# Empty slots of expert 0 written early by plain transfers instead of late by scatters, and the counts read after the last product of the first layer

## The chip, the core and the metric

The kernel runs on one NeuronCore of a Trainium2 chip. The metric is device microseconds of one execution, lower is better; a time is the median of several runs. Engines: PE (TensorE, matmul), DVE (VectorE), ACT (ScalarE), POOL (GpSimd), SP (SyncE, which here only issues transfers). Each engine runs its own instructions strictly in order and waits on semaphores.

## The reference: what is computed

```python
# stage 1, per batch b and head h (8 batches, 8 heads, 576 positions, 64 channels)
scores = q @ k.T / sqrt(64);  ret = scores * gamma_h ** (i - j) for j <= i, else 0
x = (ret @ v), heads side by side           # 4608 tokens x 512
# stage 2, a mixture of 8 experts, one expert a token
logits = x @ w_gate;  e = argmax(logits);  gate_w = softmax(logits)[e]
eom = sigmoid(x @ w_output_gate)
out[token] = gate_w * eom[e] * (relu(x @ w1[e]) @ w2[e])     # w1 512x1024, w2 1024x512
```

The kernel does the two layers of an expert as three products each, of a rounded high half and a low rest of both operands (`w1h`, `w1l`, `xh`, `xl`, `hh`, `hl`).

## The kernel before, in words

**Stage 1, the tile loop.** A loop over 36 tiles g of 128 tokens (two batches are 9 tiles). In tile g PE computes the scores of tile g+1 (`sc`), the part of the output that comes from the running state (`by_state`, `o_ps`), the part from the tile's own scores (`outT`), the state's update (`st_ps`), transposes of k for some tiles (`k_ps`), and, for tile g-1, the transposed result and the gate's logits (`xnat`, `xa` and `xb`). DVE masks the scores (`S_sb`), scales the output (`xT`), adds up logits (`lg`), does the gate, and makes the low half of expert 0's weights (`lo_w`, line 153). POOL scales v (`prep`, tile `vp`, line 364) and issues the scatters. SP loads tile g+4 (`pk`, 768 KB), rows of k (`kn`) and weights (`st`). Order within each of these engines is the order of the code (a manual schedule); a `pk` load waits until its buffer (one of 5) is free.

**The gate and the slots.** Every four tiles form a group n (9 groups). For each token the gate finds its expert and its slot: a running count `cum` per expert (over the groups so far) plus the rank within the group. Expert e owns rows e·4608 and on of a table `xs` in DRAM, 2112 bytes a row: 512 values of x, the token's number and its weight. `gate3a` makes the slots (`sli`), `gate3b` adds four scatters to a list `todo`, each writing 128 token rows to their slots (`scatter_x`); `scatters(n, pause)` takes n of them a tile and issues a small memset (`gap`) ahead of each.

**Slots that stay empty.** The MLP reads 616 slots of every expert, whatever the counts (3 tiles of up to 128, 360 slots in all, then 2 tiles of 128). A slot that got no token must hold zeros and a token number that the output scatter drops. `zx` is 128 such empty rows in SBUF. `fill` computes on DVE the numbers of the slots from the count on (all others are pushed out of range and dropped), and each fill is a scatter of `zx`. Expert 0 starts before the gate is done: its first 360 slots (part 0) hold only tokens of groups 0 to 5 (`SNAP` = 5); if the count after group 5 is below 360, later tokens start at slot 360 (`bump`, `base2`). So part 0 is filled by 3 scatters made in tile 27 (`gate4`, n == SNAP) and issued in tiles 29 and 30, and read in tile 31 (`load_rows`, `load_idx`). Three more scatters, made and issued in tile 35 (n == 7), fill expert 0's part 1, 128 slots each, and the slots of the last group, group 8, wait for them (`gt["after"]`), since its rows go over filled ones. For that count group 7 has five extra small matmuls (`c_ps`, lines 477 and 479).

**Stage 2, the experts.** For each expert the first layer `mm1(e, part, fb)` (8 blocks fb, for part 0 with 360 tokens and part 1 with 256), the second layer `mm2(e, t)` (5 token tiles), then the output scatter (line 299) on POOL. Expert 0's blocks 0 to 4 of part 0 run while the last group's gate is computed. Then come the final counts: a matmul of `cum` (line 738), its copy to `cnt` and the `fill` of all experts on DVE, the fills of experts 1 and 0 on POOL (`fill_slots`), and blocks 5 to 7. (The counts' matmul lies between two hand-ordered sections; on PE it came to stand inside block 5.) The fills of expert e+2 are issued while expert e runs. A read of `xs` waits for every scatter issued in the code ahead of it.

Of the kernel before, what the change touches and what calls it, by code (L numbers as in the profile page):

```python
# [10 lines left out]
F32 = mybir.dt.float32  # L11
# [37 lines left out]
def tile_retention_moe(  # L49
# [80 lines left out]

    wpool.tile([P, 48], F32, name="shift1")
    W1, W2 = {}, {}

    def start_w(which, e, fp):
        src, shape = (w1, [P, KB, 256]) if which == 1 else (w2, [P, 2, DM])
        st = wst.tile(shape, F32, name="st")
        SP.dma_start(out=st, in_=src[e, fp].rearrange("p (a b) -> p a b", a=shape[1]))
        hi = wpool.tile(shape, F32R, name=f"w{which}h{fp}")  # L140
        lo = wpool.tile(shape, F32R, name=f"w{which}l{fp}")
        (W1 if which == 1 else W2)[e, fp] = (hi, lo)
        return st, hi, lo
# [17 lines left out]
    xta.tile([P, 32], F32, name="shift2")  # L161
    XG, XT, HT = {}, {}, {}
    pe = [None]
    scat, todo, fillt = [], [], []
    pools = {"xt0": xta, "ht0": hpa}

    def read(paced=False, first=None, **kw):
# [31 lines left out]
    def scatter_x(x, at, bound=None):  # L199
        i = G.indirect_dma_start(out=xs, out_offset=bass.IndirectOffsetOnAxis(ap=at, axis=0), in_=x, in_offset=None,  # L200
                                 **({} if bound is None else dict(bounds_check=bound, oob_is_err=False)))
        tc.declare_no_dep(i.ins, group="xs", reason="the slots written differ, and those read so far get no more")
        tc.add_to_no_dep_group("xs", i.ins)
        scat.append(i.ins)

    def fill(e0, e1, n, lim, nj, late=False):

# [108 lines left out]
    def load(g):  # L316
        t = ld.tile([P, 3, 512], F32, name="pk")
        SP.dma_start(out=t, in_=pack[g])
        pk[g] = t
# [144 lines left out]
    def gate2(ps):  # L464

        n, oh, ex, zs = gt["pend"]
        r_ps = ps[:, 0:GT * E].rearrange("p (t e) -> p t e", t=GT)
        T.matmul(r_ps, lhsT=cbf_sb[:, 0, :], rhs=oh, start=True, stop=False, skip_group_check=True)
        if n > 0:
            T.matmul(r_ps, lhsT=cbf_sb[:, 1, :], rhs=cum.rearrange("p (a e) -> p a e", a=1).broadcast_to([P, GT, E]),  # L470
                     start=False, stop=False, skip_group_check=True)
        for t in range(GT - 1):
            T.matmul(r_ps[:, t + 1:], lhsT=cbf_sb[:, 1, :], rhs=oh[:, t:t + 1].broadcast_to([P, GT - 1 - t, E]),
                     start=False, stop=t == GT - 2, skip_group_check=True)
        c_ps = ps[:, GT * E:GT * E + E]
        if n in (SNAP, NTILE // GT - 2):
            T.matmul(c_ps, lhsT=cbf_sb[:, 1, :], rhs=cum, start=False, stop=False, skip_group_check=True)
            for t in range(GT):
                T.matmul(c_ps, lhsT=cbf_sb[:, 1, :], rhs=oh[:, t], start=False, stop=t == GT - 1, skip_group_check=True)
        gt["ps"] = (r_ps, c_ps)  # L480

    def gate3a():
        n, oh, ex, zs = gt["pend"]
        r_ps, c_ps = gt.pop("ps")
        bs = base if n <= SNAP else base2
        sl = sm.tile([P, GT, E], F32, name="sl", bufs=1)
        V.tensor_tensor(out=sl, in0=r_ps, in1=bs.broadcast_to([P, GT, E]), op=ALU.add)
        if n in (SNAP, NTILE // GT - 2):
            V.tensor_copy(cnt[:, 0], c_ps[:, 0:1])
        V.tensor_tensor(out=sl, in0=sl, in1=oh, op=ALU.mult)  # L490
        slf = sm.tile([P, GT, 1], F32, name="slf")
        V.tensor_reduce(out=slf, in_=sl, op=ALU.add, axis=AX.X)
        sli = sm.tile([P, GT, 1], I32, name="sli")
        i = V.tensor_copy(sli, slf)
        for j in gt.get("after", ()):
            tc.add_manual_dep(i.ins, j.name, SYNC, reason="the last group's rows go over filled slots")
        gt["sl"] = sli

    def gate3b():
# [16 lines left out]
    def gate3c():  # L516
        n, oh = gt.pop("cum")
        if n == 0:
            V.memset(cum, 0.0)
        ohs = sm.tile([P, E], F32, name="ohs")  # L520
        V.tensor_reduce(out=ohs, in_=oh.rearrange("p t e -> p e t"), op=ALU.add, axis=AX.X)
        V.tensor_tensor(out=cum, in0=cum, in1=ohs, op=ALU.add)
        if n in (SNAP, NTILE // GT - 2):
            gt["fill"] = n

    def gate4():
        n = gt.pop("fill")
        if n == NTILE // GT - 2:

            V.tensor_tensor(out=cnt[:, 0], in0=cnt[:, 0], in1=bump, op=ALU.add)  # L530
            todo.extend(fill(0, 1, cnt[:, 0:1], lim, CT - TA + 1)[0])
        if n == SNAP:

            todo.extend(fill(0, 1, cnt[:, 0:1], float(CA), TA)[0])
            V.tensor_scalar(out=bump, in0=cnt[:, 0], scalar1=-1.0, scalar2=float(CA), op0=ALU.mult, op1=ALU.add)
            V.tensor_scalar(out=bump, in0=bump, scalar1=0.0, scalar2=None, op0=ALU.max)
            V.tensor_copy(base2, base)
            V.tensor_tensor(out=base2[:, 0, 0:1], in0=base2[:, 0, 0:1], in1=bump, op=ALU.add)

    def xnat(g):  # L540
        xa = ps_1.tile([P, 512], F32, name="xa")
# [47 lines left out]
    def scatters(n, pause):  # L589
        for f in todo[0:n]:  # L590

            G.memset(pause, 0.0)
            f()
        del todo[0:n]

    with tc.manual_schedule():
        S_next = scores(0)
        k_rows(0)
        for g in range(NTILE):
            S_sb = S_next  # L600
            prev = stcur[0] if g % CPB != 0 else None
            if g < 4:
                load_rest(g)
            load_k(g + 1)
            if g < NTILE - 4:
                load(g + 4)
            if g == GT * SNAP + 11:
                first = list(scat)
            if g == GT * SNAP + 11:
                for t in range(TA):  # L610
                    load_rows(0, t, first)
                load_idx(0, 0, first)
            if g == 0:
                outT(g, S_sb, prev)
            if g + 1 < NTILE:
                prep(g + 1)
                S_next = scores(g + 1)
            else:
                pools["x_ps"] = k_bank
                transp(0, 2)  # L620
            if g < NTILE - 1:

                scatters(2 if GT * SNAP + 6 < g < GT * SNAP + 11 else 1, gap)
            if prev is not None:
                by_state(g, prev)
            weights(g)
            if g > 0:
                outT(g, S_sb, prev)
            update(g)
            if "pend" in gt and g % GT == 2:  # L630

                gate2(ps_s.tile([P, NP, P], F32, name="k_ps").rearrange("p a i -> p (a i)"))
            if g + 1 < NTILE:
                k_rows(g + 1)

            if "half" in gt:
                gate1b()
            if "fill" in gt:
                gate4()
            if "ps" in gt:  # L640
                gate3a()
            weights_lo(g, (0,))
            weights_lo(g - 1, (1,))
            if g > 0:
                xnat(g - 1)
            if "sl" in gt and g != NTILE - 2:
                gate3b()
            if g % GT == 0 and g > 0:
                gate1a(g // GT - 1)
            if g == NTILE - 1:  # L650
                wide = wk.tile([P, H, D], F32, name="vp")
                gate3c()
                gate4()
                scatters(len(todo), wide)
            if g in (NTILE - 3, NTILE - 2):
                if g == NTILE - 2:
                    pools["x_ps"] = lambda: sc[:, 1].rearrange("p (b k i) -> p b k i", b=2, k=2)
                x = transp_hi(0, g - NTILE + 3)
                if "sl" in gt:
                    gate3b()  # L660
                transp_lo(*x)
    gt["after"] = list(scat)
    psctx.close()
    ps_h = mctx.enter_context(tc.tile_pool(name="ps_h", bufs=4, space=PSUM, side="right", reuse_waits="tile"))
    pools["ps_h"] = ps_h
# [68 lines left out]
    hidden(*block)  # L734
    weights(NTILE)
    weights_lo(NTILE)
    c_ps = ps_t.tile([P, 512], F32, name="t_ps")[:, 0:E]
    T.matmul(c_ps, lhsT=cbf_sb[:, 1, :], rhs=cum, start=True, stop=True)
    V.tensor_copy(cnt[:, :, 0], c_ps)
    V.tensor_tensor(out=cnt[:, 0], in0=cnt[:, 0], in1=bump, op=ALU.add)  # L740
    fills = fill(0, E, cnt, lim, CT)
    fills[0] = fill(0, 1, cnt[:, 0:1], float(CAP), 1, late=True)[0]
    rest.__exit__(None, None, None)

    def fill_slots(e):
# [6 lines left out]
        load_rows(0, t)  # L752
    load_idx(0, 1)
    w = [start_w(1, 1, fp) for fp in range(2)]
    fill_slots(1)
    fill_slots(0)
    for fb in range(5, FB):
        mm1(0, 0, fb)
    load_idx(1, 0)
    load_idx(1, 1)  # L760
    mm2(0, 0)
# [164 lines left out]
```

## Time and profile before

| | |
|---|---|
| median of 3 runs | 603.85 us (603.75 to 605.16) |
| the profiled execution, its own time | 600.12 us |
| its span, first to last instruction | 598.3 us |
| granted PE clock | 0.996 |
| busy: PE, DVE, ACT, POOL | 586.4, 330.8, 227.0, 186.3 us |
| tile loop | up to about 155 us |
| scatters of token rows, of fills | 36, 42 |

In a line of the timeline stand start (us), duration (us), engine, line of the code, operation, tile written <- tiles read, shape, and, in brackets, the idle time of the engine just before and what ended it. Several like instructions in a row are merged (x16), with the duration from the first start to the last end. Ends of matmuls are modelled. In a line of the windows stand the stretch, its length, the busy time of PE, of PE's weight loads, of DVE, ACT and POOL with the number of instructions, the granted clock, the DMA share and GB/s. SPq and POOLq are the issuing sides of these engines.

### The profile page before, as it was taken

The numbers are of one execution on the slowest core, as the hardware profiler recorded it, in microseconds if no ns is written. First come the engines' busy times: TensorE is split into PE (matmuls) and PEld (weight loads), VectorE is DVE, ScalarE is ACT, GpSimd is POOL, SyncE is SP. The second block draws the span as 40 slices with busy tenths as digits, with TensorE's granted clock in tenths as the row PEclk, the third lists the DMA queues.
The fourth block names the chain that finished last, engine by engine and source line by source line (L and its number), as shares of the span: only waits on it lengthen the run. The fifth ranks groups of instructions, "written<-read, shape, count | busy, mean of one in ns | idle before, by whom it ended". The sixth has DMA issues, their size and how long they took to land. (4 is left out here: it accounts for less than half of the span.)

```text
span 598.3 us, 14014 instructions
## 1 busy us (share of the span) xinstructions
PE 586.4 (98%) x5692; PEld 525.7 (88%) x5692; DVE 330.8 (55%) x731; ACT 227.0 (38%) x502; POOL 186.3 (31%) x235
## 2 busy tenths in 40 slices
PE   8999999999999999999999999999999999999995
PEld 6889899889988999889979987997899799889974
DVE  3589899898641864626543472454355435626410
ACT  4534443334322554325333442443344234325210
POOL 3245555575655551125014102501330110110011
PEclk9999999999999999999999999999999999999998
DMA  8889889886235565326424732453273335421011
GB/s 325 293 288 322 323 299 350 328 307 202 92 118 170 173 219 149 141 67 162 172 86 129 183 122 90 125 163 110 89 181 129 121 97 151 131 77 53 1 42 39
DMA packets 54429, 98.97 MB, mean 165 GB/s; under 512 B 14903, under 2 KB 33336, under 8 KB 54364
## 3 DMA queue, kind: packets, MB, share of 16 engines
q1 hardware_dynamic: 44492, 75.42, 39.0%
q0 software_dynamic: 9440, 21.60, 9.9%
q8 instruction: 45, 0.74, 0.5%
q10 hardware_dynamic: 432, 1.05, 0.5%
q14 instruction: 20, 0.16, 0.1%
HBM read 76.45 MB, written 31.18 MB: 180 GB/s over the span
## 5 line engine op out<-in xcount | busy, mean ns | idle before, releaser
L272 PE MATMUL h_ps<-xh,w1h 128*128 128x256 f32 (+1 forms) x512 | 154.7, 302 | 0.0
L272 PE MATMUL h_ps<-xh,w1l 128*128 128x256 f32 (+1 forms) x512 | 154.5, 302 | 0.0
L272 PE MATMUL h_ps<-xl,w1h 128*128 128x256 f32 (+1 forms) x512 | 154.5, 302 | 0.0
L299 POOL DMA_INDIRECT out_dram<-y,idx x40 | 39.8, 995 | 314.3 <-ACT y L298 268.5
L280 DVE SCALAR_TENSOR_TENSOR hl<-h_ps,hh 128x256 fp32r<-128x256 f32 (+1 forms) x128 | 61.1, 477 | 129.1 <-ACT hh L279 125.7
L293 PE MATMUL y_ps<-w2h,hh 128*128 128x512 f32 (+1 forms) x320 | 125.0, 390 | 0.0
L293 PE MATMUL y_ps<-w2l,hh 128*128 128x512 f32 (+1 forms) x320 | 124.9, 390 | 0.0
L293 PE MATMUL y_ps<-w2h,hl 128*128 128x512 f32 (+1 forms) x320 | 124.7, 390 | 0.0
L279 ACT ACTIVATE hh<-h_ps 128x256 fp32r<-128x256 f32 (+1 forms) x128 | 54.8, 428 | 116.9 <-PE h_ps L272 114.8
L272 PEld LDWEIGHTS h_ps<-xh,w1l 128*128 128x128 f32 x512 | 97.1, 190 | 0.0
L272 PEld LDWEIGHTS h_ps<-xh,w1h 128*128 128x128 f32 x512 | 96.1, 188 | 0.3
L272 PEld LDWEIGHTS h_ps<-xl,w1h 128*128 128x128 f32 x512 | 96.1, 188 | 0.3
L298 ACT ACTIVATE y<-y_ps,idx 128x512 f32<-128x512 f32 (+1 forms) x40 | 27.5, 688 | 138.7 <-issue 90.1
L153 DVE TENSOR_TENSOR w1l<-st,w1h 128x512 fp32r<-128x512 f32 x64 | 47.3, 776 | 48.0 <-ACT w1h L148 46.6
L293 PEld LDWEIGHTS y_ps<-w2h,hl 128*128 128x128 f32 (+1 forms) x320 | 58.8, 184 | 14.1
L293 PEld LDWEIGHTS y_ps<-w2h,hh 128*128 128x128 f32 (+1 forms) x320 | 58.8, 184 | 13.7
L293 PEld LDWEIGHTS y_ps<-w2l,hh 128*128 128x128 f32 (+1 forms) x320 | 58.8, 184 | 13.6
L364 POOL TENSOR_TENSOR vp<-pk,con_sb 128x512 f32<-128x512 f32 x36 | 37.5, 1041 | 52.9 <-PE st_ps L404 37.4
L200 POOL DMA_INDIRECT xs<-xgrp,sli x36 | 39.1, 1087 | 29.8 <-issue 12.9
L200 POOL DMA_INDIRECT xs<-zx,fill x42 | 43.3, 1031 | 7.2 <-issue 6.5
L388 DVE TENSOR_TENSOR S_sb<-sc,con_sb 128x512 f32<-128x512 f32 x64 | 41.0, 682 | 7.4 <-PE sc L377 7.0
L153 DVE TENSOR_TENSOR w2l<-st,w2h 128x512 fp32r<-128x512 f32 x64 | 44.7, 736 | 0.0
(130 smaller groups left out, 676.1 us busy)
## 6 DMA issues: line engine op xcount, KB each, us to landing
st<-in_w_dram SPq DMA_DIRECT2D x64, 512.0 KB
pk<-in_pack_dram SPq DMA_DIRECT2D x32, 768.0 KB
x_q<-xs SPq DMA_DIRECT2D x140, 64.0 KB
kn<-in_krow_dram SPq DMA_DIRECT2D x13, 256.0 KB
pk<-in_pack_dram SPq DMA_DIRECT2D x4, 256.0 KB
pk<-in_pack_dram SPq DMA_DIRECT2D x2, 512.0 KB
x_g<-xs SPq DMA_DIRECT2D x4, 256.0 KB
xs<-zx,fill POOLq DMA_INDIRECT x42, 3.6
```

The costliest lines, as they stand in the source:

```text
L153: V.tensor_tensor(out=lo[:, k], in0=st[:, k], in1=hi[:, k].bitcast(F32), op=ALU.subtract)
L200: i = G.indirect_dma_start(out=xs, out_offset=bass.IndirectOffsetOnAxis(ap=at, axis=0), in_=x, in_offset=None, **({} if bound is None else ...
L272: i = T.matmul(ps, lhsT=a[:, k, :], rhs=b[:, k, 0:n], start=(j == 0), stop=(j == 3 * KB - 1))
L279: A.activation(out=hh, in_=ps, func=AF.Relu)
L280: V.scalar_tensor_tensor(out=hl, in0=ps, scalar=0.0, in1=hh.bitcast(F32), op0=ALU.max, op1=ALU.subtract)
L293: i = T.matmul(ps, lhsT=a[:, n], rhs=b, start=(j == 0), stop=(j == 3 * FB - 1))
L298: A.activation(out=y, in_=ps, func=AF.Copy, scale=idx.bitcast(F32)[0:m, e, t, 1:2])
L299: G.indirect_dma_start(out=out, out_offset=bass.IndirectOffsetOnAxis(ap=idx[0:m, e, t, 0:1], axis=0), in_=y, in_offset=None, bounds_check= ...
L364: G.tensor_tensor(out=vs[g], in0=pk[g][:, 2].rearrange("p (h d) -> p h d", h=H), in1=gk_sb[:, g % CPB].broadcast_to([P, H, D]), op=ALU.mult)
L388: V.tensor_tensor(out=v(S_sb[:, r].rearrange("p a i -> p (a i)")), in0=v(sc[:, r]), in1=cmat_sb[:, 0:2].rearrange("p c a i -> p a (c i)"). ...
```

## The change

Five plain transfers on SP (`empty_rows`), one in tile 3, one in tile 4, two in tile 5, one in tile 6, write `zx` over all 616 slots of expert 0. The first `gap` memset on POOL waits for all five, and so does every scatter, which stand behind it. The two sets of three fills for expert 0 go, with their DVE work, the five extra matmuls of group 7, and the last group's wait. The scatters of a tile become one where tiles 27 to 30 had two. The counts' matmul, its copy and the `fill` of all experts move behind the last `mm1(0, 0, 7)`. The one remaining fill of expert 0, for a count above its slots, stays. Two small tiles for fill numbers go, and a spacer grows by 64 bytes.

```diff
-    wpool.tile([P, 48], F32, name="shift1")
+    wpool.tile([P, 64], F32, name="shift1")
...
+    def empty_rows(t):
+
+        n = min(P, CAP - P * t)
+        i = SP.dma_start(out=xs[P * t:P * t + n], in_=zx[0:n])
+        tc.add_to_no_dep_group("xs", i.ins)
+        empty.append(i.ins)
...
-        if n in (SNAP, NTILE // GT - 2):
+        if n == SNAP:
             T.matmul(c_ps, lhsT=cbf_sb[:, 1, :], rhs=cum, start=False, stop=False, skip_group_check=True)
...
-        i = V.tensor_copy(sli, slf)
-        for j in gt.get("after", ()):
-            tc.add_manual_dep(i.ins, j.name, SYNC, reason="the last group's rows go over filled slots")
+        V.tensor_copy(sli, slf)
...
-        n = gt.pop("fill")
-        if n == NTILE // GT - 2:
-
-            V.tensor_tensor(out=cnt[:, 0], in0=cnt[:, 0], in1=bump, op=ALU.add)
-            todo.extend(fill(0, 1, cnt[:, 0:1], lim, CT - TA + 1)[0])
-        if n == SNAP:
-
-            todo.extend(fill(0, 1, cnt[:, 0:1], float(CA), TA)[0])
-            V.tensor_scalar(out=bump, in0=cnt[:, 0], scalar1=-1.0, scalar2=float(CA), op0=ALU.mult, op1=ALU.add)
...
+        gt.pop("fill")
+        V.tensor_scalar(out=bump, in0=cnt[:, 0], scalar1=-1.0, scalar2=float(CA), op0=ALU.mult, op1=ALU.add)
...
-            G.memset(pause, 0.0)
+            i = G.memset(pause, 0.0)
+            if not scat:
+                for j in empty:
+                    tc.add_manual_dep(i.ins, j.name, SYNC, reason="rows go over empty ones")
             f()
...
+            for t in {3: (0,), 4: (1,), 5: (2, 3), 6: (4,)}.get(g, ()):
+                empty_rows(t)
...
-                scatters(2 if GT * SNAP + 6 < g < GT * SNAP + 11 else 1, gap)
+                scatters(1, gap)
...
                 gate3c()
-                gate4()
                 scatters(len(todo), wide)
...
-    gt["after"] = list(scat)
...
+    for fb in range(5, FB):
+        mm1(0, 0, fb)
     c_ps = ps_t.tile([P, 512], F32, name="t_ps")[:, 0:E]
     T.matmul(c_ps, lhsT=cbf_sb[:, 1, :], rhs=cum, start=True, stop=True)
     V.tensor_copy(cnt[:, :, 0], c_ps)
     V.tensor_tensor(out=cnt[:, 0], in0=cnt[:, 0], in1=bump, op=ALU.add)
     fills = fill(0, E, cnt, lim, CT)
     fills[0] = fill(0, 1, cnt[:, 0:1], float(CAP), 1, late=True)[0]
...
     fill_slots(1)
     fill_slots(0)
-    for fb in range(5, FB):
-        mm1(0, 0, fb)
```

DVE in tile 27, between the output's scaling (`xT`) and the next masking (`S_sb`). Before:

```order
L431 TENSOR_TENSOR xT<-o_ps,gq_sb 128x512
L213 TENSOR_TENSOR fl<-cnt,csm_sb 128x3
L215 TENSOR_SCALAR fo<-fl 128x3
L223 TENSOR_TENSOR fl<-fl,fo 128x3
L224 TENSOR_TENSOR fill_2273<-fl,csm_sb 128x3
L535 TENSOR_SCALAR bump<-cnt 128x1
L536 TENSOR_SCALAR bump<-bump 128x1
L537 COPY base_84<-csm_sb 128x8
L538 TENSOR_TENSOR base_84<-base_84,bump 128x1
L153 TENSOR_TENSOR w2l_1944<-st,w2h_1943 128x512
L555 COPY lg<-xa 128x16
```

DVE at the same place, now:

```order
L438 TENSOR_TENSOR xT<-o_ps,gq_sb 128x512
L534 TENSOR_SCALAR bump<-cnt 128x1
L535 TENSOR_SCALAR bump<-bump 128x1
L536 COPY base_84<-csm_sb 128x8
L537 TENSOR_TENSOR base_84<-base_84,bump 128x1
L153 TENSOR_TENSOR w2l_1949<-st,w2h_1948 128x512
L554 COPY lg<-xa 128x16
```

The four operations that made the fill numbers are gone; the rest keeps its order.

PE at the end of block 5 and the start of block 6 of expert 0's first layer, before (`h_ps` is the layer's sum, `t_ps` here takes the counts):

```order
L272 MATMUL h_ps<-xh_2778,w1h_1014 128x360
L272 MATMUL h_ps<-xl_2779,w1h_1014 128x360
L738 LDWEIGHTS cbf_sb
L738 MATMUL t_ps<-cum,cbf_sb 128x8
L272 MATMUL h_ps<-xh_2778,w1l_1015 128x360
L272 MATMUL h_ps<-xh_2778,w1h_1330 128x360
```

PE at the end of block 7 and the start of the second layer, now:

```order
L279 MATMUL h_ps<-xh_2764,w1h_1335 128x360
L279 MATMUL h_ps<-xl_2765,w1h_1335 128x360
L279 MATMUL h_ps<-xh_2764,w1l_1336 128x360
L754 LDWEIGHTS cbf_sb
L754 MATMUL t_ps<-cum,cbf_sb 128x8
L300 MATMUL y_ps<-w2h_1632,hh_2916 128x512
```

The counts' matmul stood in front of block 5's last product; it now stands behind block 7, in front of the first product of the second layer.

SP in tiles 3 to 7, before:

```order
L318 DMA pk<-in_pack_dram 128x1536 x2
L350 DMA kn<-in_krow_dram 128x512
L318 DMA pk<-in_pack_dram 128x1536
L139 DMA st<-in_w_dram 128x1024
L318 DMA pk<-in_pack_dram 128x1536
L350 DMA kn<-in_krow_dram 128x512
L318 DMA pk<-in_pack_dram 128x1536 x2
```

SP in the same tiles, now:

```order
L325 DMA pk<-in_pack_dram 128x1536 x2
L209 DMA xs<-zx 128x528
L357 DMA kn<-in_krow_dram 128x512
L325 DMA pk<-in_pack_dram 128x1536
L209 DMA xs<-zx 128x528
L139 DMA st<-in_w_dram 128x1024
L325 DMA pk<-in_pack_dram 128x1536
L209 DMA xs<-zx 128x528 x2
L357 DMA kn<-in_krow_dram 128x512
L325 DMA pk<-in_pack_dram 128x1536
L209 DMA xs<-zx 104x528
L325 DMA pk<-in_pack_dram 128x1536
```

Each of the five writes stands behind the page of `pk` of its own tile and ahead of the next tile's loads.

More of the change, by code (lines that the diff above doesn't have):

```diff
@@ L163, in tile_retention_moe @@
     pe = [None]
-    scat, todo, fillt = [], [], []
+    scat, todo, fillt, empty = [], [], [], []
     pools = {"xt0": xta, "ht0": hpa}
@@ L487, in gate3a @@
         V.tensor_tensor(out=sl, in0=r_ps, in1=bs.broadcast_to([P, GT, E]), op=ALU.add)
-        if n in (SNAP, NTILE // GT - 2):
+        if n == SNAP:
             V.tensor_copy(cnt[:, 0], c_ps[:, 0:1])
@@ L522, in gate3c @@
         V.tensor_tensor(out=cum, in0=cum, in1=ohs, op=ALU.add)
-        if n in (SNAP, NTILE // GT - 2):
+        if n == SNAP:
             gt["fill"] = n
     def gate4():
-        n = gt.pop("fill")
-        if n == NTILE // GT - 2:
-            V.tensor_tensor(out=cnt[:, 0], in0=cnt[:, 0], in1=bump, op=ALU.add)
-            todo.extend(fill(0, 1, cnt[:, 0:1], lim, CT - TA + 1)[0])
-        if n == SNAP:
-            todo.extend(fill(0, 1, cnt[:, 0:1], float(CA), TA)[0])
[L535 to L538, printed above, removed]
+        gt.pop("fill")
+        V.tensor_scalar(out=bump, in0=cnt[:, 0], scalar1=-1.0, scalar2=float(CA), op0=ALU.mult, op1=ALU.add)
+        V.tensor_scalar(out=bump, in0=bump, scalar1=0.0, scalar2=None, op0=ALU.max)
+        V.tensor_copy(base2, base)
+        V.tensor_tensor(out=base2[:, 0, 0:1], in0=base2[:, 0, 0:1], in1=bump, op=ALU.add)
     def xnat(g):
@@ L736, in tile_retention_moe @@
     weights_lo(NTILE)
[L737 to L742, printed above, removed]
     rest.__exit__(None, None, None)
@@ L754, in tile_retention_moe @@
     w = [start_w(1, 1, fp) for fp in range(2)]
+    for fb in range(5, FB):
+        mm1(0, 0, fb)
+    c_ps = ps_t.tile([P, 512], F32, name="t_ps")[:, 0:E]
+    T.matmul(c_ps, lhsT=cbf_sb[:, 1, :], rhs=cum, start=True, stop=True)
+    V.tensor_copy(cnt[:, :, 0], c_ps)
+    V.tensor_tensor(out=cnt[:, 0], in0=cnt[:, 0], in1=bump, op=ALU.add)
+    fills = fill(0, E, cnt, lim, CT)
+    fills[0] = fill(0, 1, cnt[:, 0:1], float(CAP), 1, late=True)[0]
     fill_slots(1)
     fill_slots(0)
-    for fb in range(5, FB):
-        mm1(0, 0, fb)
     load_idx(1, 0)
```

## The prediction

> **What bounds the kernel now.** I read the busy times first, then the windows for stretches in which PE is not full, then the timeline at those places. Columns of a window: stretch, length, busy PE, PE's loads, DVE, ACT, POOL, clock, DMA share, GB/s.
>
> ```profile
> PE 586.4 (98%) x5692; PEld 525.7 (88%) x5692; DVE 330.8 (55%) x731; ACT 227.0 (38%) x502; POOL 186.3 (31%) x235
> ...
> 120.00:140.00 20.00, 19.02 (x426) 16.96 (x426) 18.37 (x55) 7.94 (x21) 14.50 (x22) 1.00 0.84 285
> ...
> 160.00:180.00 20.00, 18.89 (x110) 17.40 (x109) 10.04 (x43) 5.41 (x14) 13.34 (x17) 1.00 0.33 122
> ```
>
> PE sets the time: whatever it does not wait for costs nothing. It waits in only a few places. The start and the last 9 us aside, the two largest are the missing 0.98 us in 120:140 and 1.11 us in 160:180. Both lie beside work that the change removes or moves. The second thing to see is that in the tile loop DVE is 18.4 of 20 us busy and the DMA share is 0.84, so little can be added there.
>
> **Tile 27: four operations leave DVE.**
>
> ```profile
> 104.03 0.68 DVE L431 TENSOR_TENSOR xT<-o_ps,gq_sb 128x512 f32<-128x512 f32 x1
> 112.05 0.68 DVE L431 TENSOR_TENSOR xT<-o_ps,gq_sb 128x512 f32<-128x512 f32 x1
> ...
> 119.70 1.01 POOL L200 DMA_INDIRECT xs<-xgrp,sli  x1 [2.79 <-issue]
> ...
> 120.34 0.68 DVE L431 TENSOR_TENSOR xT<-o_ps,gq_sb 128x512 f32<-128x512 f32 x1
> ...
> 120.94 0.15 DVE L213 TENSOR_TENSOR fl<-cnt,csm_sb 128x3 f32<-128x3 f32 x1
> 121.32 1.76 DVE L223 TENSOR_TENSOR fl<-fl,fo 128x3 f32<-128x3 f32 x1
> 122.00 1.05 POOL L364 TENSOR_TENSOR vp<-pk,con_sb 128x512 f32<-128x512 f32 x1
> 123.17 0.63 PE L404 MATMUL st_ps<-vp,kn 128*64 128x64 f32 x16
> 123.20 0.15 DVE L535 TENSOR_SCALAR bump<-cnt 128x1 f32<-128x1 f32 x1
> 123.72 0.69 DVE L153 TENSOR_TENSOR w2l<-st,w2h 128x512 fp32r<-128x512 f32 x1
> 124.33 0.17 DVE L555 COPY lg<-xa 128x16 f32<-128x16 f32 x1
> 124.55 0.76 PE L546 MATMUL xa<-iw,xT 128*128 128x144 f32 x4 [0.75 <-DVE lg L555]
> 126.03 0.90 PE L377 MATMUL sc<-pk 64*64 64x128 f32 x32 [0.23 <-DVE S_sb L388]
> ...
> 129.20 0.68 DVE L431 TENSOR_TENSOR xT<-o_ps,gq_sb 128x512 f32<-128x512 f32 x1
> ```
>
> The fill numbers of part 0 take DVE from 120.94 to 123.20, 2.26 us, of which 1.76 us is one operation on 128x3 values that ends when POOL's `vp` ends (123.05). The logits' copy (`lg`) comes 2.26 us late for it, and PE, which has one `xa` buffer, stands 0.75 us and then 0.23 us. Upper bound of the gain: 0.98 us. Lower bound from the rhythm: two tiles from 120.34 to 129.20 take 8.86 us, two from 104.03 to 112.05 take 8.02 us, so 0.84 us too much. I take 0.9 us: with the operations gone PE can go on at its own pace, since only 0.98 of DVE's 2.26 us are needed.
>
> What is late next: the rest of the bump (four operations of about 0.15 us) and the weights' low half, 0.69 us, reading two SBUF tiles. POOL issues one scatter instead of two here, so its next `vp` starts about 120.75, straight behind the first scatter, and ends at 121.8, in the middle of the bump. If the bump's last operation or the low half stands until then, `lg` starts at 121.8 + 0.15 + 0.69 = 122.6, still 1.7 us before 124.33.
>
> [...]
>
> **The last group: a wait and a matmul go from PE's path.**
>
> ```profile
> 164.19 0.99 POOL L200 DMA_INDIRECT xs<-zx,fill  x1 [0.17 <-issue]
> 167.10 0.19 DVE L492 TENSOR_REDUCE slf<-sl 128x4 f32<-128x32 f32 x1
> 168.42 0.17 DVE L494 CAST sli<-slf 128x4 int32<-128x4 f32 x1 [1.14 <-DMA xs<-zx,fill]
> 169.41 0.17 DVE L522 TENSOR_TENSOR cum<-cum,ohs 128x8 bf16<-128x8 bf16 x1
> ...
> 168.20 0.33 PE L272 MATMUL h_ps<-xl,w1h 128*128 128x360 f32 x1
> 169.63 0.18 PE L738 MATMUL t_ps<-cum,cbf_sb 128*128 128x8 bf16 x1 [1.11 <-DVE cum L522]
> ```
>
> The last fill by scatter, issued at 164.19, holds the slots' cast (`sli`) for 1.14 us; `cum` is ready at 169.6, and the counts' matmul in the middle of block 5 stands for it. Products follow each other every 0.165 us, so the next was due at 168.36 and the stall is 1.27 us by starts (1.11 us by the profile's modelled ends). Both causes go: without the fills `cum` comes at 168.3, and the matmul stands behind block 7, at about 172.4, where it waits for nothing. I take 1.2 us, with 1.11 and 1.27 as ends. The matmul itself costs the same at either place.
>
> ```profile
> 150.55 0.17 PE L477 MATMUL k_ps<-cum,cbf_sb 128*128 128x8 bf16 x1
> ...
> 150.68 0.74 PE L546 MATMUL xa<-iw,xT 128*128 128x144 f32 x4
> ```
>
> Group 7's five count matmuls go: from 150.55 to 150.68, 0.13 us of PE. The six DVE operations of tile 35 go for nothing, for PE was in block 0 and 1 meanwhile.
>
> **The fills that move back.** The fill numbers of all experts now wait for block 7.
>
> ```profile
> 173.28 0.20 DVE L223 TENSOR_TENSOR fl<-fl,fo 128x40 f32<-128x40 f32 x1
> 174.07 0.47 ACT L279 ACTIVATE hh<-h_ps 128x360 fp32r<-128x360 f32 x1 [1.50 <-PE h_ps L272]
> 174.30 0.96 POOL L200 DMA_INDIRECT xs<-xgrp,sli  x1 [0.30 <-issue]
> 175.56 1.00 POOL L200 DMA_INDIRECT xs<-zx,fill  x1 [0.30 <-DVE hl L280]
> ...
> 193.24 0.38 SPq L139 DMA_DIRECT2D st<-in_w_dram  x1
> 199.97 0.61 ACT L148 CAST w1h<-st 128x512 fp32r<-128x512 f32 x1
> ```
>
> Block 7's `hh` comes at 174.07 - 1.25 = 172.8, its `hl` at about 173.7, then copy, bump and five operations of 0.2 us: the numbers are there at 175.0. POOL's last scatter of token rows now ends at 175.26 - 1.14 = 174.1, so the first fill starts about 175.2 instead of 175.56. In time it is no later; against PE, which is 1.25 us earlier, it is 0.9 us later. Behind the six fills on POOL stand the first output scatters, for which nobody waits soon, and on SP the reads of expert 1's rows and the weights issued at 193.24. Those are cast at 199.97: 6.7 us later, against 512 KB, which at the 285 GB/s of 120:140 are 1.8 us, and a landing. 0.9 us is covered; cost nothing. From about 3 us on each microsecond of delay would come back as one on PE.
>
> **The five writes at the start.** They are 616 rows of 2112 bytes, 1.3 MB, on SP's queue.
>
> ```profile
> q0 software_dynamic: 9440, 21.60, 9.9%
> ...
> 20.00:36.00 16.00, 15.64 (x344) 13.86 (x336) 11.20 (x28) 6.84 (x23) 3.43 (x4) 1.00 0.70 240
> 36.00:60.00 24.00, 24.00 (x516) 21.68 (x514) 21.97 (x64) 9.85 (x27) 14.06 (x19) 1.00 0.91 322
> ...
> POOL vp L364 <- DMA pk<-in_pack_dram: 8.8, 3, 5.2
> ...
> 22.73 0.78 SPq L318 DMA_DIRECT2D pk<-in_pack_dram  x1
> 30.89 3.56 SPq L318 DMA_DIRECT2D pk<-in_pack_dram  x2
> 35.70 1.04 POOL L364 TENSOR_TENSOR vp<-pk,con_sb 128x512 f32<-128x512 f32 x1 [4.08 <-issue]
> 39.39 1.15 POOL L200 DMA_INDIRECT xs<-xgrp,sli  x1 [2.62 <-PE o_ps L428]
> ...
> DMA to landing us min/median/max: 2.1/4.4/6.7
> ```
>
> The nearest row is the scatter queue's: 9.9% of 16 engines over 598.3 us for 9440 packets is 100 ns each, of 2288 bytes. 616 of them on 16 engines are 3.9 us. The stretch 20:36, in which tiles 4 to 6 lie, leaves the engines idle for 0.30 of 16 us = 4.8 us, so the queue can take it there. Where the idle time comes too early, a page is late by some 1.5 us; the page of tile 8, issued at 22.73, is first used by `vp` at 35.70, 13 us later. Cost nothing; upper end 3.9 us if the loads have no slack.
>
> The new wait: the first `gap` on POOL. The last write is issued right behind the page at 30.89, at about 31.3. With the landing times of this kernel's scatters (2.1 to 6.7 us) it is done by 33.4 to 38.0; the scatter behind the `gap` starts only at 39.39, held by its rows. Behind it on POOL stands the next `vp`. Covered by 1.4 us in the worst case; cost nothing, upper end some 0.5 us. SP's own issue, five times about 0.4 us (0.38 in the row at 193.24), costs nothing: of the 3.56 us from 30.89, with two issues, most is waiting.
>
> **Sum.** 0.9 + 1.2 + 0.13 = 2.2 us, plus nothing. The span of 598.3 becomes 596.1, the profiled execution's 600.12 becomes 597.9. That execution was 3.7 us below the median of the runs shown, 603.85, so I carry the difference over: 601.6 us, 0.37% faster. A measurement of this kernel can tell about 0.3% (1.8 us) from no change.
>
> **Rivals.**
>
> [...]
> - The start pays (the other side). The DMA engines are 0.91 busy in 36:60 and 0.84 in 120:140; if every later page comes 3.9 us later and no page has slack, the loop ends 3.9 us later, tile 27's gain is hidden by it, and 603.85 + 3.9 - 1.3 = 606.4, 0.43% slower. It decides from the point at which a page lands after its `vp` is due, 13 us from issue. Against it: in the whole loop `vp` waited for a page three times, 8.8 us together.
> - More than forecast: one scatter a tile in 27 to 30 also frees `vp` and the low halves there. Four tiles there, at the pace of 8.02 us for two, would be another 0.7 us: 600.5 or lower.
>
> **How the numbers follow.** Forecast 0.60 (600.8 to 602.2, from 0.84 and 1.11 to 0.98, 1.27 and 0.13, with half a us of scatter between runs), gain given back 0.19, start pays 0.09, more 0.08, fills too late for expert 1 0.04 (603 to 605). Range 600.4 to 603.2: it leaves out the slow cases and part of "more", 0.16. Faster by over 0.3% (below 602.04): most of the forecast and all of "more", 0.61. Same: the rest of the forecast, the gain given back, some of the late fills, 0.29. Slower: 0.10.
>
> **What would show it.** After: no PE wait for `cum`, and the cast of the last group's slots behind its reduce without a gap; PE full in the stretch of tiles 27 and 28; the first `gap` on POOL ending before 39 us and the scatter behind it where it was; `vp` waiting for `pk` no more often than before; the first fill of expert 1 near 174 to 175 us. Wrong would be a tile loop that ends later than before, or a new PE wait for `lg` or `S_sb` after tile 27.

## The result, and the profile after

The changed kernel takes 612.44 us (612.08 to 612.71), the kernel before 604.5 us beside it: ratio 1.0134 [1.012, 1.0148], 1.3% or some 8 us slower. Forecast were 601.6 us. The profiled execution of after: own time 612.67 us, span 610.8 us, granted clock 0.989.

The page and two windows of after, as shown of before:

```profile
PE 591.4 (97%) x5687; PEld 528.6 (87%) x5687; DVE 328.5 (54%) x720; ACT 226.0 (37%) x502; POOL 178.8 (29%) x223
...
q0 software_dynamic: 8960, 21.33, 9.5%
...
120.00:140.00 20.00, 19.79 (x405) 17.36 (x404) 17.64 (x55) 7.60 (x21) 9.62 (x14) 1.00 0.85 304
160.00:180.00 20.00, 20.00 (x128) 19.36 (x127) 10.56 (x42) 6.61 (x16) 9.86 (x12) 1.00 0.25 96
```

In the two stretches that the prediction spoke of, PE is now almost full (19.79 and 20.00 for 19.02 and 18.89), as forecast. Every wait of PE that was to go is gone. These are PE's longest waits now, with total, number and longest:

```profile
PE o_ps L426 <- issue: 1.6, 7, 0.4
PE sc L561 <- DVE zx L558: 1.5, 1, 1.5
PE k_ps L365 <- DMA con_sb<-in_cmat_dram: 0.2, 1, 0.2
```

Neither `cum` nor `lg` stands there. So the time was lost where PE does nothing. The windows of the last 20 us, before (span 598.3) and after (span 610.8):

```profile
580.00:590.00 10.00, 10.00 (x46) 8.24 (x45) 0.00 (x0) 1.38 (x2) 2.01 (x2) 1.00 0.15 49
590.00:598.00 8.00, 1.19 (x6) 0.65 (x4) 0.00 (x0) 0.69 (x1) 0.98 (x1) 0.71 0.06 23
```

```profile
590.00:600.00 10.00, 5.17 (x23) 3.94 (x21) 0.00 (x0) 1.19 (x2) 1.99 (x2) 0.87 0.12 45
600.00:610.00 10.00, 0.00 (x0) 0.00 (x0) 0.00 (x0) 0.00 (x0) 0.00 (x0) 0.50 0.00 1
```

In the last 10 us of after no engine is busy and next to nothing moves (1 GB/s), and still the program is not over. What runs there is seen only among the instructions that are not counted as busy. These are the last scatter (timeline) and the last instructions of POOL's sequencer (least/median/largest ns, first start to last start), of before:

```profile
592.24 0.98 POOL L299 DMA_INDIRECT out_dram<-y,idx  x1 [4.44 <-ACTq L818]
L818 POOLq INC_SWDGE_SEM  x1: 408/408/408, 592.7 to 592.7; - x1
L922 POOLq DRAIN  x3: 40/103/1047, 596.4 to 598.0; - x3
```

and of after:

```profile
596.22 0.98 POOL L306 DMA_INDIRECT out_dram<-y,idx  x1 [4.44 <-ACTq L820]
L820 POOLq INC_SWDGE_SEM  x1: 2398/2398/2398, 596.7 to 596.7; - x1
L924 POOLq DRAIN  x3: 40/103/9214, 600.8 to 610.6; - x3
```

The longest of POOL's three final `DRAIN`s grew from 1.05 to 9.21 us. The `INC_SWDGE_SEM` behind the last scatter grew by 2.0 us, but lies mostly beside that scatter's landing (it runs from 596.7 to 599.1, the scatter's packets move until 598.4 to 598.8): the drains begin 3.20 us after the scatter's end before (593.22 to 596.42) and 3.60 us after it now (597.21 to 600.81). 8.16 + 0.40 = 8.56 us. The two ends agree: from the last matmul's start to the end of the span it is 7.5 us before (590.80 to 598.3), 16.0 us after (594.78 to 610.8), 8.5 us more.

The other 4.0 us of the 12.5 us between the two spans lie ahead of the last matmul, and most of them are put down to the chip. The record does not name the chips of these two profiles, but before's own time there, 600.1 us, is that of the faster chips of the runs below, and after was timed beside a before of 604.5 us, as on the slower ones. The runs below have both kernels on both kinds.

### The profile page after: what moved, and what is told of

Its sections match the earlier page's. It is cut to its first block, busy times and chain, and to the rows that moved or that the text cites. A ratio compares the mean times of both kernels' runs of the same rounds, so it can differ in the third digit from the quotient of the medians.

```text
span 610.8 us, 13978 instructions
## 1 busy us (share of the span) xinstructions
PE 591.4 (97%) x5687; PEld 528.6 (87%) x5687; DVE 328.5 (54%) x720; ACT 226.0 (37%) x502; POOL 178.8 (29%) x223
## 3 DMA queue, kind: packets, MB, share of 16 engines
q0 software_dynamic: 8960, 21.33, 9.5%
q10 hardware_dynamic: 432, 1.05, 0.5%
## 5 line engine op out<-in xcount | busy, mean ns | idle before, releaser
L153 DVE TENSOR_TENSOR w1l<-st,w1h 128x512 fp32r<-128x512 f32 x64 | 45.7, 751 | 48.0 <-ACT w1h L148 46.7
L435 PE MATMUL o_ps<-S_sb,vp 128*64 128x128 f32 x576 | 40.3, 279 | 0.1
```

The costliest lines, as they stand in the source:

```text
L153: V.tensor_tensor(out=lo[:, k], in0=st[:, k], in1=hi[:, k].bitcast(F32), op=ALU.subtract)
L435: T.matmul(part(p, r), lhsT=vs[g][:, 2 * p + r, :], rhs=S_sb[:, r, p, :], start=(state is None and p < 2), stop=True, skip_group_check=True)
```

## The experiments

"Transfers" below are the indirect ones (`indirect_dma_start`, the scatters). The page counts them: 9440 packets on queue q0 before are 118 transfers of 80, 8960 after are 112. A dummy transfer has all its row numbers out of range, moves no row, and stands behind the fills of expert 7, which are issued while expert 5 runs; a spacer is cut so that the addresses stay. Each figure for "final DRAIN" is the longest of the three.

| kernel | transfers | final DRAIN, us | median, us | ratio to before on the same chip |
|---|---|---|---|---|
| a_less30 | 82 | 6.76 | 609.85 (1 run) | 1.01 |
| after | 112 | 9.21 | 612.44 | 1.0134 [1.012, 1.0148] |
| a_pad12 | 112 | 9.21 | 607.56 | 1.0126 [1.0108, 1.0143] |
| b_less6 | 112 | 9.22 | 613.43 | 1.0139 [1.0119, 1.016] |
| a_plus1 | 113 | 9.30 | 612.37 | 1.011 [1.0093, 1.0127] |
| a_plus2 | 114 | 0.72 | 604.79 (one of its 10 runs took 2048.24) | 1.0002 [0.9988, 1.0015] |
| a_plus4 | 116 | 0.88 | 597.83 | 0.9964 [0.995, 0.9978] |
| a_plus6 | 118 | 1.05 | 603.95 | 0.9973 [0.9959, 0.9987] |
| a_plus8 | 120 | 1.21 | 603.31 | 0.9972 [0.9958, 0.9987] |
| b_same, b_empty, b_one_row | 118 | 1.05 | 599.83, 599.9, 599.98 | 0.9994, 1.0003, 1.0008 |
| b_plus2 | 120 | 1.21 | 604.83 | 0.9999 [0.9986, 1.0012] |
| a_plus4_2row | 112 + 4 of 2 rows | 9.55 | 612.29 | 1.0125 [1.0102, 1.0149] |
| a_plus6_2row | 112 + 6 of 2 rows | 9.71 | 608.46 (1 run) | 1.01 |
| a_plus9_2row | 112 + 9 of 2 rows | 0.73 | 599.22 (1 run) | 1.00 |

**Are the five writes to blame?** Before with the writes and the first gap's wait, but all its scatters (b_empty); the same with one row in each write (b_one_row); and before as it is, for the spread (b_same).

```diff
+            for t in {3: (0,), 4: (1,), 5: (2, 3), 6: (4,)}.get(g, ()):
+                empty_rows(t)
```

and in b_one_row, within `empty_rows`:

```diff
-        n = min(P, CAP - P * t)
+        n = 1
```

> The kernel before, unchanged, to see how far two executions of it differ. The profile of before has its last matrix product at 590.8 us and then 7.1 us to the end, of which POOL's last wait for its own pipeline is 1.05 us; the changed kernel has 15.6 us behind its last product, of which that wait is 9.2 us. If the end is a property of the program, this run has 7.1 us again and the loop ends (last scaling of an output) at 154.5 us. If the end varies from run to run, 3 to 6 us of the difference between the profiled 600.12 and the other runs of before (603.75 to 605.18) are found there.

> Before, with the five plain writes of empty rows added in tiles 3 to 6 and the first scatter's wait for them; all fills stay where they were. The changed kernel's tile loop ends 5.3 us later than before (159.8 against 154.5). Theory W (the bytes of the writes move the page loads against PE): the loop ends near 160 and the time is about 604.5 + 5.3 = 609.8. Theory L (any five more transfers in SP's queue do it, bytes or not): the same 609.8. Theory E (the loop is slower for something else in the change): the loop ends near 154.5, the time is 604 to 605.

> The same five transfers at the same places, each of one row of 2112 bytes instead of up to 128 rows, so 10 KB instead of 1.3 MB; fills as before, so the result of the computation is whole. Theory W: no bytes, no loss, the loop ends near 154.5, 604 to 605 us. Theory L: the loop ends near 160, about 609.8. Theory E: 604 to 605.

Measured 599.83, 599.9 and 599.98 us: b_empty 1.0003 [0.9994, 1.0013], b_one_row 1.0008 [0.9991, 1.0024]. POOL's last drains of b_empty:

```profile
L934 POOLq DRAIN  x3: 40/103/1047, 597.4 to 599.0; - x3
```

The writes, with or without their 1.3 MB, leave the end as it was and are not to blame for the 8 us. In the time they cost nothing that can be told from zero; 0.8 us (the upper end for b_empty) is not excluded.

**Does the shifted code change the end?** After with 12 more memsets on POOL ahead of expert 7's fills, as many instructions as POOL lost (223 for 235).

```diff
+        for _ in range(12 if e == 7 else 0):
+            G.memset(gap, 0.0)
```

> The changed kernel with twelve one-element memsets on POOL ahead of the last fills, where POOL is idle: POOL then has about as many instructions as in the kernel before, with the same 112 indirect transfers as the changed kernel. At the end of the changed kernel a page of 8 KB of instructions is fetched 0.2 us into POOL's last wait, which lasts 9.2 us; in before the fetch lies 1.7 us ahead of that wait, which lasts 1.05 us. Theory P (the page of instructions falls into the end): the last wait shrinks to about 1 us and the time to about 612.4 - 8.2 = 604.2. Theory C (the number of indirect transfers, 112 against 118): the last wait stays near 9 us and the time near 612.4.

607.56 us, 1.0126, and the drain is the same:

```profile
L926 POOLq DRAIN  x3: 40/103/9214, 596.5 to 606.3; - x3
```

The last 8 KB of instructions are now fetched at 595.97 us, 0.6 us ahead of the drain (in after at 601.0, inside it), and the drain is as long. The place of the code is not the cause.

**Is it the number of transfers?** Dummies in after (1, 6, 8), and in before (2).

```diff
+    far = const.tile([P, 1], I32, name="far")
+    G.memset(far, 2 * E * NT)
...
-        for f in fills[e]:
+        for f in fills[e] + [partial(scatter_x, zx, far, E * NT - 1)] * (6 if e == E - 1 else 0):
```

> The changed kernel with one more indirect transfer on POOL (all of its row numbers out of range, so it writes nothing), issued with the fills of the last expert, where POOL is idle: 113 in all. The transfers go round eight semaphores; the end increments the semaphore that would be next. In the changed kernel (112) that is the first of the eight, in before (118) the seventh. Theory 8 (the end is long when the count is a multiple of eight): POOL's last wait is about 1 us, the time 1.0126 x before less 8.5 us, so about 0.9 us below before. Theory N (the end is long below some count between 112 and 118): the wait stays 9.2 us, 1.3% slower than before. Theory S (it lies in what else the change does): also 9.2 us.

> The same with six more indirect transfers, 118 as in before. Theory 8: short end, about 0.9 us below before. Theory N: short end, the same. Theory S: long end, 9.2 us, 1.3% slower than before.

> The same with eight more, 120, again a multiple of eight. Theory 8: long end, 9.2 us, 1.3% slower than before. Theory N: short end, about 0.9 us below before. Theory S: long end.

> The kernel before with two more such transfers, 120 in all; nothing else of the change is in it. Theory 8: POOL's last wait grows from 1.05 to about 9.2 us and the kernel gets 8 to 8.5 us slower than before (1.4%). Theories N and S: the end stays short and the time that of before.

a_plus1, a_plus6, a_plus8, b_plus2, one line of each:

```profile
L927 POOLq DRAIN  x3: 40/103/9296, 600.4 to 610.2; - x3
```

```profile
L927 POOLq DRAIN  x3: 40/103/1047, 602.1 to 603.7; - x3
```

```profile
L927 POOLq DRAIN  x3: 40/103/1211, 600.5 to 602.3; - x3
```

```profile
L925 POOLq DRAIN  x3: 40/103/1211, 601.9 to 603.6; - x3
```

One more transfer makes the drain 0.08 us longer; six more make it 8.2 us shorter, and the kernel faster than before. 120 transfers give 1.21 us in either kernel, 118 give 1.05 us in either, so it is the number and nothing else of the change. A rule by multiples of eight falls: 118 is none and is short, 112 is one and is long. There is a border between 113 and 118.

**Where is the border, and must it be this change?** Two dummies in after (a_plus2); after without the output scatters of experts 1 to 6, which leaves their rows of `out` unwritten (a_less30); before without those of expert 3 and the first of expert 4 (b_less6), which leaves those rows unwritten; and four transfers that carry two row numbers each (a_plus4_2row).

```diff
+        if e in (0, E - 1):                 # a_less30
+        if e != 3 and (e, t) != (4, 0):     # b_less6
             G.indirect_dma_start(out=out, ...
...
-    partial(scatter_x, zx, far, E * NT - 1)
+    partial(scatter_x, zx[0:2], far[0:2], E * NT - 1)   # a_plus4_2row
```

> The changed kernel with two more indirect transfers that write nothing, 114 in all. So far POOL's last wait was 9.21 us at 112 transfers and 9.30 at 113 (0.082 us for each transfer since the start), and 1.05 at 118 and 1.21 at 120 (0.08 us each from about the 105th on). In the runs with 118 and 120 the 114th comes 1.5 us late. [...] Theory M (the border lies at 115 to 118): the last wait is 9.4 us, 1.1% slower than before.

> The changed kernel without the output scatters of experts 1 to 6, 82 indirect transfers (the output rows of these experts are not written). [...] Theory F (below the border the end costs the same whatever the number): 9.2 us.

> The kernel before, nothing of the change in it, without the output scatters of expert 3 and the first of expert 4, so 112 indirect transfers (those output rows are not written). [...] Theory S (the end is long for something else in the change): 1.05 us, and the time of before.

> The changed kernel with four more indirect transfers, 116 in all, but of two rows each instead of 128. Theory T (the number of transfers counts): past the border, last wait about 0.9 us, 0.27% faster than before. [...]

a_plus2, a_less30, b_less6, a_plus4_2row:

```profile
L927 POOLq DRAIN  x3: 40/103/721, 601.0 to 602.3; - x3
```

```profile
L925 POOLq DRAIN  x3: 40/103/6764, 600.4 to 607.7; - x3
```

```profile
L923 POOLq DRAIN  x3: 45/103/9222, 601.8 to 611.6; - x3
```

```profile
L927 POOLq DRAIN  x3: 45/103/9549, 600.2 to 610.3; - x3
```

The border lies between 113 (9.30) and 114 (0.72). Below it the drain grows with the transfers, from none: (9214 - 6764) / 30 = 82 ns each, and 6764 / 82 = 82.5 ns each. So up to 113 the drain is as long as 82 ns for every transfer since the start, and behind the border as for 8 or 9 of them (721 / 82 = 8.8 at 114, 14.8 at 120). Before falls off the same edge once it loses six transfers of its own (613.43 us), with none of the change in it. And 112 + 4 short transfers, 116 in all, stay long: towards the border a short transfer counts for less than a full one, while the drain counts by transfers (9549 / 116 = 82.3 ns).

The 114th transfer itself starts late. It is the last of a_plus2:

```profile
597.24 0.99 POOL L306 DMA_INDIRECT out_dram<-y,idx  x1 [5.91 <-issue]
```

5.91 us of idle for the 4.44 us of the last scatter in after: 1.5 us, on the path here, which is why a_plus2 only equals before (1.0002). In a_plus8 the 114th is an earlier output scatter, and the 1.5 us are hidden: the scatter behind it waits for its `y` again, 2.95 us:

```profile
538.34 1.01 POOL L306 DMA_INDIRECT out_dram<-y,idx  x1 [5.92 <-issue]
542.30 0.99 POOL L306 DMA_INDIRECT out_dram<-y,idx  x1 [2.95 <-ACT y L305]
```

**How much does a short transfer count towards the border?** After with 6 and with 9 short transfers, and, as the version to keep, with 4 full dummies.

```diff
-    ... * (4 if e == E - 1 else 0):
+    ... * (6 if e == E - 1 else 0):     # a_plus6_2row; 9 in a_plus9_2row
```

> The changed kernel with six more indirect transfers of two rows, 118 in all. [...] Theory T2 (any transfer counts as one, but those of two rows not at all): 9.7 us.

> The same with nine transfers of two rows, 121 in all. [...] Theory T2: 121 x 0.082 = 9.9 us.

> The changed kernel with four more indirect transfers of 128 rows that write nothing, 116 in all, issued where POOL is idle. The 114th is then the third from last and its 1.5 us lie beside PE's work; the last wait is (116 - 105) x 0.08 = 0.9 us. The rest of the change should show alone: tile 27 to 35 1.2 to 1.4 us shorter, the last group 1.2 us, the counts' matmul 0.1 us back, the five writes 0 to 1 us: 0.9965 to 0.9985 of before. If the change is worth nothing without its end, 1.000.

a_plus6_2row, a_plus9_2row (with its last scatter), a_plus4:

```profile
L927 POOLq DRAIN  x3: 45/103/9712, 596.1 to 606.4; - x3
```

```profile
592.23 0.99 POOL L306 DMA_INDIRECT out_dram<-y,idx  x1 [5.99 <-issue]
L927 POOLq DRAIN  x3: 45/103/729, 595.9 to 597.2; - x3
```

```profile
L927 POOLq DRAIN  x3: 40/103/884, 594.0 to 595.5; - x3
```

Six short transfers stay below the border, nine cross it with the very last scatter, late by the same 1.5 us. Measured is only this: 113 full stay below the border and 114 do not; 112 full and 6 short stay below; 112 full and 9 short do not, though without the last transfer, a full one, they still did. If the shares simply add up, an estimate from these four counts is that a short transfer takes between a ninth and a third of a full one: far more than its 2 rows of 128, so it is not the rows alone that count. Why the border lies there is not shown.

a_plus4, with 116 transfers, took 597.83 us against 600.06 us on the same chip, 0.9964 [0.995, 0.9978]: 2.2 us [1.3, 3.0] faster than before, and the version that beats both. In a_plus6, which has before's own number of 118, the rest of the change shows on its own: 0.9973, 1.6 us [0.8, 2.5].

## Why the prediction was wrong

The step that failed is the sentence "The start and the last 9 us aside": no term was made for the end, and the transfers removed were counted only by their work on DVE and POOL, "PE sets the time: whatever it does not wait for costs nothing". The last 7.5 us are set by no PE. Six transfers fewer took the kernel from 118 to 112, below a border at 114, and the end from 7.5 to 16.0 us. Where the border lies can't be read from the one profile of before; but its rows did show a final drain that no busy engine, no DMA and no line of the chain accounts for, and a term for the end, however wide, would have had to be in the range. In the light of the runs one more row of before speaks: ahead of its 114th transfer, the fifth from the end, POOL stands idle for 32.77 us and the profile names no cause for the end of it; ahead of the scatter at the same place in after, the 108th there, it is 1.47 us less:

```profile
571.85 0.99 POOL L299 DMA_INDIRECT out_dram<-y,idx  x1 [32.77 <-issue]
574.36 0.98 POOL L306 DMA_INDIRECT out_dram<-y,idx  x1 [31.30 <-ACT y L305]
```

The rival on the other side was the wrong one: the start did not pay the 3.9 us named there.

Of the two signs named for a wrong forecast, no new wait of PE came. A later end of the tile loop did: tile 35's `xT` is at 159.80 in after, 154.51 before. Most of that is the chip, not the change: on one and the same chip it is at 155.53 in a_pad12, 155.75 in b_empty and 154.28 in b_same, which has no writes, and 159.80 stands beside 160.26 in b_plus2, before with two dummies on a chip of the slower kind.

Terms of the sum, first on a_plus4, since its profile (span 595.7) stands on a chip like that of before (598.3), then on the others:

- **Tile 27, 0.9 us and 0.13 us: about right as a balance.** From tile 27's `xT` to tile 35's: 34.17 us before (120.34 to 154.51), 33.27 us in a_plus4 (120.26 to 153.53), 0.90 us less, the five count matmuls included. The timeline of a_plus4:

```profile
120.26 0.68 DVE L438 TENSOR_TENSOR xT<-o_ps,gq_sb 128x512 f32<-128x512 f32 x1
120.66 1.05 POOL L371 TENSOR_TENSOR vp<-pk,con_sb 128x512 f32<-128x512 f32 x1
121.10 0.66 DVE L536 COPY base<-csm_sb 128x8 f32<-128x8 f32 x1
121.87 0.75 DVE L153 TENSOR_TENSOR w2l<-st,w2h 128x512 fp32r<-128x512 f32 x1
122.55 0.16 DVE L554 COPY lg<-xa 128x16 f32<-128x16 f32 x1
123.64 0.76 PE L545 MATMUL xa<-iw,xT 128*128 128x144 f32 x4
```

`vp` starts at 120.66 (forecast 120.75), `lg` at 122.55 (forecast 122.6), and `xa` stands for nothing. The copy of 128x8 values to `base` takes 0.66 us, 0.16 us before, and ends about when `vp` ends (121.71); the low half behind it has 0.75 us for the 0.69 us before. So one operation ended with `vp`, as the one of 1.76 us had before, and not one that I had named; why it did is in no trace.

The "gain given back" of the chances (0.19, the author's estimate that tile 27's gain is lost again in the tiles behind it) happened in part, within the 0.90 us. From `xT` to `xT`, tile 27 to 28 took 3.85 us for 5.55, 1.70 us less, more than the 0.98 us named as the upper bound; then 28 to 31 took 12.13 for 11.49 and 31 to 32 took 3.82 for 3.55, 0.91 us more; and 34 to 35, without the count matmuls, 3.56 for 3.68. That the balance came near the forecast is in part luck. The other profiles scatter about it: tile 27 to 35 takes 34.16 to 35.01 us in the four kernels with all their fills on the faster chips and 33.27 to 33.82 us in the four changed ones; on the slower chips 36.67 and 36.70 us against 35.45 to 35.56 us.

- **The last group, 1.2 us: right in the mean.** Block 4's `hh` to block 5's is 2.20 us in after and in every kernel with the counts behind block 7; it was 3.60 us in the profile of before, and 3.03 us (b_less6) to 3.69 us (b_same) in the other five kernels with the counts inside block 5. That is 0.8 to 1.5 us. After's cast follows its reduce without a gap and the counts' matmul waits for nothing:

```profile
172.39 0.19 DVE L499 TENSOR_REDUCE slf<-sl 128x4 f32<-128x32 f32 x1
172.61 0.17 DVE L501 CAST sli<-slf 128x4 int32<-128x4 f32 x1
...
177.77 0.18 PE L754 MATMUL t_ps<-cum,cbf_sb 128*128 128x8 bf16 x1
```

Moved behind block 7 it costs 0.09 us of PE (block 7 to the second layer 5.63 us for 5.54), where I had said the same at either place.

- **The fills that move back, nothing: right.** The first fill of expert 1 starts 2.74 us after block 7's `hh` (177.96 to 180.70 in after), before 1.49 us: 1.25 us later against PE for the 0.9 us forecast, and covered. From block 8's `hh` to the last token tile PE needs 398.39 us in before, after and a_plus4 alike.

- **The writes and the first gap, nothing: not settled, up to about 1 us.** In after the first gap ends at 39.50, later than the 39 forecast, held until 39.41 by what the profile calls a DMA, but the scatter behind it is held by its rows still:

```profile
39.41 0.09 POOL L591 MEMSET gap<- 1x1 f32 x1 [3.34 <-DMA pk<-in_pack_dram]
40.30 1.24 POOL L200 DMA_INDIRECT xs<-xgrp,sli  x1 [0.80 <-PE xb L545]
```

`vp` waited for `pk` three times, 9.3 us together, before three times, 8.8 us (in a_plus4 four times, 10.2 us). But tile 27's `xT` comes later in the kernels with the writes: at 120.3 to 121.9 us on the faster chips, where before and b_same have 120.3 and 119.3, and at 123.6 to 126.0 us on the slower, where b_less6 and b_plus2 have 123.4 and 123.6; on average 1.0 to 1.3 us. These are single profiles, whose first `xT` alone lies between 8.8 and 10.7 us. b_empty may understate it: there PE's wait for `cum` is still in place, and it shrank to 0.88 us from 1.20 in b_same, so that part of a later loop is hidden.

- **The sum: too large.** 2.2 us were forecast. In the profile of a_plus4 it comes out, 0.90 + 1.4 - 0.09 = 2.2 us, and in its timed runs too, but a_plus4 is the best case of ten. For each changed kernel with whole output, take how much longer its end is than the 7.5 us of before (last matmul's start to the end of the span) and subtract how much longer its median is than before's on its chip. What is left is what the rest of the change gained: 0.6 us in after, 0.9 in a_pad12, 0.7 to 2.0 in the other eight (two of them single runs), 1.2 us in the mean. For b_less6 and b_plus2, which have nothing of the change, the same sum leaves -0.1 and 0.3 us. So some 1 us of the 2.2 is missing; the later start above would fit, but no run shows that it is the cause. After, too, is the sum of both: 8.6 us lost at the end, less 0.6 us gained ahead of it, are the 7.9 us by which its median is longer. The sum was one of the middle of the program, and the change also took away something at which nobody had looked.

## What to carry to other kernels

Account for the whole span, the stretch behind the last busy instruction included: set the last matmul, the last transfer and the last `DRAIN` against the end of the span, before and after. Where a change adds or removes indirect transfers, count them (packets of the software queue); up to 113 of 128 rows each one cost 0.08 us at the end here (a_less30, after, a_plus1), and a kernel just below 114 gained 8 to 9 us on one chip from a few empty transfers, put where their queue is idle (a_plus1 against a_plus6 and a_plus8). And compare profiles only with a run of the other kernel on the same chip, and more than one: the best of ten comparisons here bears out the forecast of 2.2 us, and their mean is 1.2 us.

## What the runs showed of the hardware that was not expected

- The final drain: 0.082 us for each indirect transfer of 128 rows up to 113 (6.76 us at 82, 9.30 at 113), and from the 114th on, which starts 1.5 us late (a_plus2, a_plus8), 0.08 us for each beyond about the 105th (0.72 us at 114, 1.21 at 120). These are counts and times alone; what happens there is not shown. The `INC_SWDGE_SEM` ahead of it goes the same way: 1.80 us at 82 transfers (a_less30), 2.40 at 112 (after), 0.32 at 114 (a_plus2). Whether the drain can be made short by other means was not tried.
- Chips differ: before took 599.9 and 600.1 us in two of the comparisons and 604.5 to 605.0 us in the three others. The difference lies in the tile loop of either kernel (tile 27 to 35: 33.3 us in a_plus4, 35.5 us in after; 34.2 us in before, 36.7 us in b_plus2). Two rows of the waits in after, of PE's weight loads that stand without a named cause:

```profile
PEld o_ps L435 <- issue: 5.2, 29, 0.3
PEld o_ps L426 <- issue: 3.9, 10, 0.5
```

In most tiles the products of `by_state` (L426) take 0.35 us from the first start to the last. They take more than 0.4 us, up to 1.2 us, in 11 to 14 of 32 tiles in the profiles on the slower chips, after's among them, and in none or one on the faster. The cause stays open.
